# ReLU-squared attention and a SwiGLU feed-forward on one core: 64x64 tiles for gate, value and score products

## The chip, the cores and the metric

The kernel runs on one core of a Trainium2 chip. The metric is device time in microseconds (us) of one execution; lower is better. The engines of the core run side by side: PE (TensorE, matrix products into PSUM), DVE (VectorE), ACT (ScalarE), POOL (GpSimd) and SP (SyncE, which here only starts transfers). PE has two kinds of instruction, a weight load (PEld in the profile) and a matmul (PE).

A matmul here multiplies a stationary operand (`lhsT`, loaded as weights) with a moving one (`rhs`) and writes `lhsT.T @ rhs`. It need not fill PE's 128x128 array. The rows it takes are the partitions of its operands, the columns are the partitions of its output. A 64x128 tile takes half of the rows and all of the columns, so two of them, one on the upper rows and one on the lower rows, can run at the same time. A 64x64 tile takes a quarter of the array, and four can run at the same time.

## The reference, cut to what matters

```python
# q, k, v: (8, 12, 448, 64) float32: batch, heads, sequence, head dimension
scores = scale * np.matmul(q, k.transpose(0, 1, 3, 2))
attn = np.maximum(scores, 0.0) ** 2 / S
a = np.matmul(attn, v)
x = a.transpose(0, 2, 1, 3).reshape(B * S, H * D)      # 3584 x 768
xn = x / np.sqrt(np.mean(x * x, axis=-1, keepdims=True) + 1e-6) * rms_g
g = xn @ w_gate                                         # 768 -> 1536
silu = g * (1.0 / (1.0 + np.exp(-g)))
out = (silu * (xn @ w_val)) @ w_out                     # 1536 -> 768
```

## The kernel before

Everything is computed in bfloat16 with float32 sums. The eight batches follow each other. While the feed-forward part of batch b runs, the attention of batch b+1 is worked in between, unit by unit. Batch 0's attention has nothing to be put beside and comes first, with some filler matmuls (`keep_busy`, psB).

**Attention units** (`attention`). `scores` makes the products of one chunk of 128 keys for two heads. The head dimension is 64, so each head takes one half of the rows: two matmuls on 64x128 tiles with 448 columns, into psS (line 212 of the profile). `rest_scores` (line 227) makes the last 64 keys of two pairs of heads on four 64x64 tiles. `rectify` takes ReLU on ACT or DVE and the square on DVE. `attend` makes attention times V for two pairs of heads into psAV on four 64x64 tiles (line 258): a first pass of four steps, `rest_scores` for another pair between the passes in most calls, then a second pass of three steps that adds to what the first pass wrote from the other half of the rows. An empty instruction with a dependence on the first pass's matmuls stands ahead of the second, so that the two halves do not add to the same place at once.

**The feed-forward part** is a list of groups. `projection` is a gate or value product of 128 hidden features for 448 tokens: six steps (KT) over the 768 inputs, into a PSUM buffer psP. `outproj` makes three `Piece`s for 128 tokens, each of 256 output columns and twelve steps (FT), into psO. `norm_sums` (psSS) has the shape of a projection and makes the sums of squares for the next batch. All of these are written by one line, 380, in `Group.emit`.

Each group of n steps is cut at its contraction: a step has an upper half (partitions 0 to 63 of the operands, upper rows of the array) and a lower half (partitions 64 to 127, lower rows), so each group needs 2n matmuls that add into the same PSUM buffer. `Stream.step` issues one **slot**: at most one matmul for the upper half of a group called *lead*, and one for the lower half of another group called *follow*. A gate or value group usually does its six upper halves first, as lead, and then its six lower halves, as follow, while the next group leads. A group that changes from one half to the other must not have both in PE at once. Two things see to it: `ready` refuses a group that changes its half before `APART` = 2 steps have gone by, and `emit` places an empty instruction (`nc.tensor.nop`) that depends on the group's last matmul. In the built program that dependence is a semaphore wait on the weight load that comes next.

```python
        def ready(self, half):
            if self.last not in (None, half) and self.rest < stream.APART:
                return False
            return self.count[half] < (self.count[0] if half else self.bound())
```

`rest` is set to 0 by a group's own slot and goes up by one at the end of every slot, so between a group's last upper half and its first lower half there is at least one slot of other groups. A `Piece` does its twelve steps in two runs of six upper and six lower halves. A slot may hold two groups of different kinds, for example psSS as lead and psO as follow.

**Order.** `manual_schedule` keeps the order in which the code issues instructions on each engine. The main loop spreads the next batch's attention units over the slots of the current batch by a list of costs. When a group has all its steps, ACT makes SiLU of a gate (line 451), DVE multiplies it with the value (line 456), and ACT copies psO out (line 490), from where SP stores it.

Of the kernel before, what the change touches and what calls it, by code (L numbers as in the profile page):

```python
# [20 lines left out]
def kernel(  # L21
# [11 lines left out]
    nc = tc.nc  # L33
    P = nc.NUM_PARTITIONS
    B, H, S, D = q.shape
    T, DM = out.shape
    _, F = moe_w_gate.shape
    assert (T, DM) == (B * S, H * D) and 2 * D == P and S % NCH == 0 and B % 2 == 0 and S == U * D
    PC = S // NCH
    KT, FT, HP = DM // P, F // P, H // 2  # L40
# [23 lines left out]
    qkT = {}  # L64
# [3 lines left out]
    def load(nm, b, h0=0, h1=H):  # L68
        runs = nm == "v" or b < PE_T
        n, w = (PC, NCH) if nm == "q" else (P, UH)  # L70
        if (nm, b) not in ld:
            shape = [n, H, w * D] if runs else [n, w, H * D]
            ld[nm, b] = ldpool.tile(shape, BF16, name=nm + "b", tag=nm + "b")
            if nm == "k" and runs:
                nc.vector.memset(ld[nm, b][D:, :, (UH - 1) * D :], 0.0)
        t = ld[nm, b]
        src = src_of[nm][b, h0:h1]
        if nm == "q":
            parts = [(slice(0, PC), PC, 0, NCH)]
        else:  # L80
            parts = [(slice(0, D), D, 0, UH), (slice(D, P), D, UH if nm == "k" else UH - 1, U)]
        for prt, n, u0, u1 in parts:
            if runs:
                nc.gpsimd.dma_start(  # L84
                    out=t[prt, h0:h1, : (u1 - u0) * D],
                    in_=src.rearrange("h (p u) d -> p h (u d)", p=n)[:, :, u0 * D : u1 * D],
                )
            else:
                to = t[prt].rearrange("p u (h d) -> p u h d", d=D)
                rows = src.rearrange("h (p u) d -> p u h d", p=n)  # L90
                step = u1 - u0 if nm == "q" else 1
                for u in range(u0, u1, step):
                    nc.gpsimd.dma_start(  # L93
                        out=to[:, u - u0 : u - u0 + step, h0:h1, :], in_=rows[:, u : u + step]
                    )
# [70 lines left out]
    behind = mybir.DependencyInfo(mybir.DependencyClass.Sync, mybir.DependencyReason.DATA)  # L166
# [30 lines left out]
    def rectify(b, j, c, psS):  # L197
        r = apool.tile([P, 2, S], BF16, name="r", tag="r")
        if relu_on(b, j, c) == "dve":
            nc.vector.tensor_relu(out=r[:], in_=psS[:, :, :S])  # L200
        else:
            nc.scalar.activation(out=r[:], in_=psS[:, :, :S], func=ACT.Relu)  # L202
        eng = nc.gpsimd if square_on(b, j, c) == "pool" else nc.vector
        flush()
        pending.append(lambda: eng.tensor_tensor(out=r[:], in0=r[:], in1=r[:], op=ALU.mult))  # L205
        rsq[b, j, c] = r

    def scores(b, j, c):
        psS = ps_s.tile([P, 2, 512], FP32, name="psS", tag="psS")
        for hh in range(2):  # L210
            prt = slice(hh * D, (hh + 1) * D)
            nc.tensor.matmul(  # L212
                out=psS[:, hh, :S],
                lhsT=qkT[b][prt, j, 0, c * P : (c + 1) * P],
                rhs=qkT[b][prt, j, 1, :],
                start=True,
                stop=True,
            )
        rectify(b, j, c, psS)

    def rest_scores(b, j):
# [59 lines left out]
    def attention(b):  # L281
        units = []

        def add(cost, *fns):
            units.append((cost, lambda: [f() for f in fns]))

        if b < PE_T:
            add(0.4, lambda: transposes(b, 0))
            add(0.4, lambda: transposes(b, 1))
            add(0.3, lambda: rectify(b, 0, UH - 1, rest_scores(b, 0)))  # L290
        for j in range(HP):
            for c in range(UH - 1):
                if c == 2 and j in (2, 4):
                    add(1.6, lambda j=j: attend(b, j - 2, (b, j)))
                add(0.3, lambda j=j, c=c: scores(b, j, c))
                if c == 1 and b < PE_T and j + 2 < HP:
                    add(0.4, lambda j=j: transposes(b, j + 2))
                if b == 0:
                    add(0.3, lambda: keep_busy(1))
        add(0.1, flush)  # L300
        add(1.6, lambda: attend(b, HP - 2, (b + 1, 0) if PE_T <= b + 1 < B else None), flush)
        return units
# [3 lines left out]
    class Stream:  # L306
# [28 lines left out]
        def step(self):  # L335
            if not (self.todo or self.open):
                return False
            lead = self.pick(0, None)
            follow = self.pick(1, lead)
            for half, g in ((0, lead), (1, follow)):  # L340
                if g is not None:
                    g.emit(half)
            self.at = [lead, follow]
            for g in self.open:
                g.rest += 1
            if follow is not None and follow.count[1] == follow.n:
                self.open.remove(follow)
                follow.done(follow.ps)
            return True
# [7 lines left out]
    class Group:  # L357
# [14 lines left out]
        def begin(self):  # L372
            self.ps = ps_m.tile([P, 512], FP32, name=self.name, tag="mm")

        def emit(self, half):
            i = self.count[half]
            prt = slice(half * D, (half + 1) * D)
            if self.last not in (None, half):
                tc.add_manual_dep(nc.tensor.nop().ins, self.mm.name, behind)
            mm = nc.tensor.matmul(  # L380
                out=self.ps[:, : self.w], lhsT=self.lhsT(i)[prt], rhs=self.rhs(i)[prt],
                start=(half == 0 and i == 0), stop=(half == 1 and i == self.n - 1),
            )
            self.count[half] += 1
            self.last, self.rest = half, 0
            self.mm = mm.ins

    class Piece(Group):

# [190 lines left out]
```

## Time and profile before

Three runs took 466.82, 468.20 and 469.97 us. One execution was profiled:

| | us or share |
|---|---|
| median of the runs | 468.2 |
| span of the profiled execution, first to last instruction | 466.5 |
| matmuls and weight loads on PE | 5722 each |
| psP matmuls, 64x128 tiles, 448 columns | 2268 (1140 value, 1128 gate), 0.349 each |
| psO matmuls, 64x128 tiles, 256 columns | 2016, 0.271 each |
| psS matmuls on 64x128 tiles | 288, 0.358 each |
| psAV matmuls, 64x64 tiles | 672, 0.361 each |
| psS matmuls on 64x64 tiles | 96, 0.360 each |
| mean weight load, 64x128 | 0.094 |
| mean weight load, 64x64 | 0.106 |

The duration of a matmul in the profile is from its start to the modelled end of its result. Matmuls overlap: the next on the same rows starts before the one ahead of it has ended, so the time of a slot is read from starts, not from durations. A line of the timeline gives start, length, engine, line of the kernel, operation, output and inputs, shape, and how many instructions of the same kind were merged into it; brackets at its end give idle time before it and what ended it. In "64*128 64x448" the first pair is the tile on the array, the second the partitions and columns of the moving operand. "PEld" lines are weight loads; a load with a wait appears when the wait is over.

### The profile page before, as it was taken

How to read it: one execution, taken by the hardware profiler on the slowest of the kernel's cores; microseconds unless marked ns; L12 is line 12 of the kernel's file. 1: busy time of each engine (PE TensorE's matmuls, PEld its weight loads, DVE VectorE, ACT ScalarE, POOL GpSimd, SP SyncE). 2: the span in 40 equal slices, each digit the busy share in tenths (PEclk: the TensorE clock that was granted, in tenths of full speed). 3: DMA queues.
4: the chain of work that ended last, by engine and by line, in shares of the span. 5: the costliest groups of instructions: out<-in, count | busy, mean ns of one | idle time of the engine just before them, and what ended most of it. 6: DMA issues, size and time to landing. Idle time of an engine off the chain costs nothing.

```text
span 466.5 us, 12798 instructions
## 1 busy us (share of the span) xinstructions
PE 453.6 (97%) x5722; PEld 292.8 (63%) x5722; DVE 274.0 (59%) x403; ACT 234.9 (50%) x360; POOL 80.6 (17%) x97
## 2 busy tenths in 40 slices
PE   6989999999999999999999999999999999999995
PEld 3434655676666766676666766676667766676674
DVE  1676378866663867576566657576656677332200
ACT  1682246665645655375445755465535764532221
POOL 8438211571007000340007000100000000000000
PEclk8698999999999999999999999999999999999998
DMA  9999999799907970299209960438002200020013
GB/s 106 194 204 199 206 173 162 80 204 165 127 3 107 214 124 2 23 200 146 44 1 124 211 109 1 58 82 135 20 1 54 85 2 1 2 84 20 1 42 95
DMA packets 130758, 44.47 MB, mean 95 GB/s; under 512 B 102928, under 2 KB 127120, under 8 KB 130704
## 3 DMA queue, kind: packets, MB, share of 16 engines
q0 software_dynamic: 91648, 24.39, 54.1%
q1 hardware_dynamic: 39056, 19.28, 20.5%
q8 instruction: 44, 0.72, 0.6%
q14 instruction: 10, 0.08, 0.0%
HBM read 48.76 MB, written 11.01 MB: 128 GB/s over the span
## 4 chain that ended last, share of the span: by engine, by line
PE 91%; DVE 3%; ACT 2%; DMA 1%; POOL 1%; issue 1%; POOLq 0%
PE psP L380 47%; PE psO L380 23%; PE psAV L258 8%; PE psS L212 6%; PE psSS L380 2%; ACT r L202 2%; PE psB L140 1%; PE psT L177 1%; PE psS L227 1%; DMA kb<-in_k_dram 1%; DVE xn L427 1%; PE psP L441 1%; DVE r L200 1%; DVE r L205 1%; DVE rstd L424 1%
## 5 line engine op out<-in xcount | busy, mean ns | idle before, releaser
L380 PE MATMUL psP<-xn,wv_sb 64*128 64x448 bf16 x1140 | 229.0, 349 | 0.0
L380 PE MATMUL psP<-xn,wg_sb 64*128 64x448 bf16 x1128 | 227.8, 349 | 0.1
L380 PE MATMUL psO<-wo_sb,hT 64*128 64x256 bf16 x2016 | 139.6, 271 | 0.0
L202 ACT ACTIVATE r<-psS 128x896 bf16<-128x896 f32 x123 | 111.1, 918 | 47.5 <-PE psS L212 46.8
L380 PEld LDWEIGHTS <-wv_sb 64*128 64x128 bf16 x1140 | 96.1, 94 | 41.5 <-issue 4.3
L380 PEld LDWEIGHTS <-hT 64*128 64x128 bf16 x2016 | 101.1, 94 | 33.0 <-issue 2.9
L380 PEld LDWEIGHTS <-wg_sb 64*128 64x128 bf16 x1128 | 94.3, 94 | 35.6 <-issue 1.3
L205 DVE TENSOR_TENSOR r<-r 128x896 bf16<-128x896 bf16 x165 | 100.9, 628 | 16.3 <-ACT r L202 15.6
L456 DVE TENSOR_TENSOR hT<-sil,psP 128x448 bf16<-128x448 bf16 x96 | 59.5, 620 | 79.7 <-PE psP L380 52.4
L451 ACT ACTIVATE sil<-psP 128x448 bf16<-128x448 f32 x96 | 51.9, 542 | 74.7 <-PE psP L380 68.8
L200 DVE TENSOR_SCALAR r<-psS 128x896 bf16<-128x896 f32 x45 | 49.1, 1090 | 31.7 <-PE psS L227 24.2
L212 PE MATMUL psS<-qkT 64*128 64x448 bf16 x288 | 59.3, 358 | 1.9 <-DVE r L200 1.2
L490 ACT COPY ost<-psO 128x256 f32<-128x256 f32 x84 | 30.5, 372 | 43.5 <-PE psO L380 39.6
L276 ACT ACTIVATE xT<-psAV 128x896 bf16<-128x896 f32 x24 | 22.0, 917 | 54.4 <-PE psAV L258 50.1
L258 PE MATMUL psAV<-r,vb 64*64 64x448 bf16 x672 | 43.9, 361 | 1.8 <-POOL r L205 1.2
L84 POOL DMA_DIRECT2D vb<-in_v_dram x18 | 13.2, 750 | 167.7 <-PE psO L380 122.3
L424 DVE RECIPROCAL rstd<-rstd 128x448 f32<-128x448 f32 x8 | 23.6, 2953 | 26.0 <-ACT rstd L420 26.0
L93 POOL DMA_DIRECT2D kb<-in_k_dram x42 | 33.0, 1008 | 18.7 <-DMA wo_sb<-in_moe_w_out_dram 9.6
L258 PEld LDWEIGHTS <-vb 64*64 64x64 bf16 x672 | 17.3, 106 | 22.3 <-issue 10.3
L427 DVE SCALAR_TENSOR_TENSOR xn<-xT,g_sb,rstd 128x448 bf16<-128x448 bf16 x48 | 29.3, 680 | 0.3
L212 PEld LDWEIGHTS <-qkT 64*128 64x128 bf16 x288 | 19.8, 94 | 11.4 <-issue 6.2
L140 PE MATMUL psB<-busy_bf,ones_bf 128*128 128x448 bf16 x58 | 17.6, 418 | 1.3 <-DVE busy_bf L135 1.3
(38 smaller groups left out, 161.7 us busy)
## 6 DMA issues: line engine op xcount, KB each, us to landing
vb<-in_v_dram POOLq DMA_DIRECT2D x14, 384.0 KB, 7.2
qb<-in_q_dram POOLq DMA_DIRECT2D x7, 672.0 KB, 12.9
kb<-in_k_dram POOLq DMA_DIRECT2D x43, 96.0 KB, 12.7
out_dram<-ost SPq DMA_DIRECT2D x8, 336.0 KB, 4.1
wg_sb<-in_moe_w_gate_dram POOLq DMA_DIRECT2D x4, 576.0 KB, 16.5
wv_sb<-in_moe_w_val_dram POOLq DMA_DIRECT2D x4, 576.0 KB, 18.1
wo_sb<-in_moe_w_out_dram POOLq DMA_DIRECT2D x2, 1152.0 KB, 21.4
out_dram<-ost SPq DMA_DIRECT2D x8, 288.0 KB, 4.4
```

The source lines that it names most:

```text
L93: nc.gpsimd.dma_start(out=to[:, u - u0 : u - u0 + step, h0:h1, :], in_=rows[:, u : u + step])
L200: nc.vector.tensor_relu(out=r[:], in_=psS[:, :, :S])
L202: nc.scalar.activation(out=r[:], in_=psS[:, :, :S], func=ACT.Relu)
L205: pending.append(lambda: eng.tensor_tensor(out=r[:], in0=r[:], in1=r[:], op=ALU.mult))
L212: nc.tensor.matmul(out=psS[:, hh, :S], lhsT=qkT[b][prt, j, 0, c * P : (c + 1) * P], rhs=qkT[b][prt, j, 1, :], start=True, stop=True,)
L258: mm = nc.tensor.matmul(out=psAV[hh * D : (hh + 1) * D, jj, :S], lhsT=v[prt, 2 * (j + jj) + hh, u * D : (u + 1) * D], rhs=r[prt, hh, :], s ...
L380: mm = nc.tensor.matmul(out=self.ps[:, : self.w], lhsT=self.lhsT(i)[prt], rhs=self.rhs(i)[prt], start=(half == 0 and i == 0), stop=(half = ...
L424: nc.vector.reciprocal(out=rstd[:], in_=rstd[:])
L427: nc.vector.scalar_tensor_tensor(out=xn[:, kt, :], in0=xTs[b][:, kt, :], scalar=g_sb[:, kt : kt + 1], in1=rstd[:], op0=ALU.mult, op1=ALU.mult,
L451: nc.scalar.activation(out=s[:], in_=psG[:], func=ACT.Silu)
L456: nc.vector.tensor_tensor(out=hTs[b // 2][:, fb, o : o + S], in0=sil[b, fb][:], in1=psV[:], op=ALU.mult)
L490: nc.scalar.copy(out=ost[:, o : o + w], in_=ps[:, :w])
```

## The change

The `scores` products and every slot that contains a gate, a value or a sum-of-squares group are issued as 64x64 tiles: each matmul of 128 output rows becomes two, one for output partitions 0 to 63 and one for 64 to 127. Within a slot the order is: first block of lead, first block of follow, second block of lead, second block of follow. Slots of output projection alone stay on two 64x128 tiles, and so do the scores that come between them: the flag `quarters` holds what the last slot was. An output projection that shares its slot with a psP or psSS group is quartered too.

`emit` is divided into three. `ordered` places the empty instruction for a change of halves, `emit` the matmul of one block, `emitted` keeps the count. `step` calls `ordered` for lead and follow, then `emit` for all blocks, then `emitted`. The last matmul that the dependence names is that of the second block.

```diff
--- before.py
+++ after.py
@@ -205,17 +205,23 @@
         pending.append(lambda: eng.tensor_tensor(out=r[:], in0=r[:], in1=r[:], op=ALU.mult))
         rsq[b, j, c] = r
 
+    quarters = [True]
+
+    def blocks():
+        return ((0, D), (D, P)) if quarters[0] else ((0, P),)
+
     def scores(b, j, c):
         psS = ps_s.tile([P, 2, 512], FP32, name="psS", tag="psS")
-        for hh in range(2):
-            prt = slice(hh * D, (hh + 1) * D)
-            nc.tensor.matmul(
-                out=psS[:, hh, :S],
-                lhsT=qkT[b][prt, j, 0, c * P : (c + 1) * P],
-                rhs=qkT[b][prt, j, 1, :],
-                start=True,
-                stop=True,
-            )
+        for m0, m1 in blocks():
+            for hh in range(2):
+                prt = slice(hh * D, (hh + 1) * D)
+                nc.tensor.matmul(
+                    out=psS[m0:m1, hh, :S],
+                    lhsT=qkT[b][prt, j, 0, c * P + m0 : c * P + m1],
+                    rhs=qkT[b][prt, j, 1, :],
+                    start=True,
+                    stop=True,
+                )
         rectify(b, j, c, psS)
 
     def rest_scores(b, j):
@@ -337,9 +343,15 @@
                 return False
             lead = self.pick(0, None)
             follow = self.pick(1, lead)
-            for half, g in ((0, lead), (1, follow)):
-                if g is not None:
-                    g.emit(half)
+            pair = [(half, g) for half, g in ((0, lead), (1, follow)) if g is not None]
+            quarters[0] = any(g.n == KT for _, g in pair)
+            for half, g in pair:
+                g.ordered(half)
+            for m in blocks():
+                for half, g in pair:
+                    g.emit(half, *m)
+            for half, g in pair:
+                g.emitted(half)
             self.at = [lead, follow]
             for g in self.open:
                 g.rest += 1
@@ -372,18 +384,23 @@
         def begin(self):
             self.ps = ps_m.tile([P, 512], FP32, name=self.name, tag="mm")
 
-        def emit(self, half):
+        def ordered(self, half):
+            if self.last not in (None, half):
+                tc.add_manual_dep(nc.tensor.nop().ins, self.mm.name, behind)
+
+        def emit(self, half, m0, m1):
             i = self.count[half]
             prt = slice(half * D, (half + 1) * D)
-            if self.last not in (None, half):
-                tc.add_manual_dep(nc.tensor.nop().ins, self.mm.name, behind)
             mm = nc.tensor.matmul(
-                out=self.ps[:, : self.w], lhsT=self.lhsT(i)[prt], rhs=self.rhs(i)[prt],
+                out=self.ps[m0:m1, : self.w], lhsT=self.lhsT(i)[prt, m0:m1],
+                rhs=self.rhs(i)[prt],
                 start=(half == 0 and i == 0), stop=(half == 1 and i == self.n - 1),
             )
+            self.mm = mm.ins
+
+        def emitted(self, half):
             self.count[half] += 1
             self.last, self.rest = half, 0
-            self.mm = mm.ins
 
     class Piece(Group):
 
```

## Prediction

> **What bounds the kernel now.** I read the page first: the busy shares (part 1), the granted clock, then the chain that ended last (part 4).
>
> ```profile
> span 466.5 us, 12798 instructions
> PE 453.6 (97%) x5722; PEld 292.8 (63%) x5722; DVE 274.0 (59%) x403; ACT 234.9 (50%) x360; POOL 80.6 (17%) x97
> PE 91%; DVE 3%; ACT 2%; DMA 1%; POOL 1%; issue 1%; POOLq 0%
> ```
>
> 91% of the chain is PE; of it psP (gate and value) is 47% and psO (output projection) 23%. DVE and ACT have 40 and 50% of slack. So the question is how long one *slot* of PE takes, and whether the change touches that. The chain in order of time, in a gate/value stage, says how long it is (start, length, what):
>
> ```profile
> 160.51 1.32 PE psP L380 x14
> 161.84 0.19 PE psS L212 x2
> 162.02 1.32 PE psP L380 x14
> 163.35 0.19 PE psS L212 x2
> ```
>
> Fourteen psP matmuls are seven slots of two: 1.32/7 = 0.189 us a slot. A score slot takes 0.19 too. The windows view grants a clock of 1.00 from 40 us to the end; 448 columns at 0.189 us is as fast as any row of this trace streams, and psO's 256 columns keep the same proportion with 0.109. Next, the timeline of PE around one attention-times-V, the only place where four 64x64 tiles run now:
>
> ```profile
> 165.98 0.35 PE L380 MATMUL psP<-xn,wv_sb 64*128 64x448 bf16 x1
> 166.03 0.35 PE L380 MATMUL psP<-xn,wg_sb 64*128 64x448 bf16 x1
> 166.31 0.95 PE L258 MATMUL psAV<-r,vb 64*64 64x448 bf16 x16
> 167.09 0.36 PE L227 MATMUL psS<-qkT 64*64 64x448 bf16 x4
> 167.32 0.79 PE L258 MATMUL psAV<-r,vb 64*64 64x448 bf16 x12
> 168.04 0.36 PE L380 MATMUL psP<-xn,wv_sb 64*128 64x448 bf16 x1
> 168.05 0.36 PE L380 MATMUL psP<-xn,wg_sb 64*128 64x448 bf16 x1
> 168.25 0.35 PE L380 MATMUL psP<-xn,wv_sb 64*128 64x448 bf16 x1
> ```
>
> Four 4-tile slots run from 166.31 to 167.09, 0.78 us: three at 0.19 and a first one of 0.21. So a slot costs the same with two tiles or four. Around them stand the switches: 166.03 to 166.31 is 0.28 where a slot is 0.19, and 0.02 more on the first slot; going back, 12 matmuls are three slots, so the last starts near 167.76, and 167.76 to 168.04 is again 0.28. A switch of tile shape costs about 0.10 to 0.11 us. And 167.09 to 167.32 is 0.23, not 0.19: the second pass of attention-times-V waits for the matmuls of the first, with one slot between.
>
> Last, what a wait for the other half's matmuls costs in the stream. First the timeline of a psP group going over (lines from PE and PEld), then psO's in three short windows:
>
> ```profile
> 160.31 0.35 PE L380 MATMUL psP<-xn,wg_sb 64*128 64x448 bf16 x1
> 160.71 0.09 PEld L380 LDWEIGHTS <-wg_sb 64*128 64x128 bf16 x1
> 160.73 0.35 PE L380 MATMUL psP<-xn,wg_sb 64*128 64x448 bf16 x1
> ...
> 406.22 0.62 PE L380 MATMUL psO<-wo_sb,hT 64*128 64x256 bf16 x8
> 406.56 0.10 PEld L380 LDWEIGHTS <-hT 64*128 64x128 bf16 x2
> ...
> 407.24 0.10 PEld L380 LDWEIGHTS <-hT 64*128 64x128 bf16 x2
> ```
>
> The gate group's last upper-half matmul starts at 160.31; the held weight load of its lower half goes at 160.71, 0.40 to 0.41 later (0.35 of matmul and some 0.06 to be told). In psO it is 406.22 to 406.56: 0.33 to 0.34. Two slots are 0.378 and 0.218: the release comes later than the slot that wants it. Today this is nearly free, because only the lower half is held and it runs behind the upper one: by 0.04 us in psP (165.98 against 166.03 above), by a whole slot in psO. psO's held loads return every 0.68 us, six slots, against 6 x 0.109 = 0.655: 0.025 a wait, the load that comes late. In psP the 1.32 us stretches contain such waits and show no loss.
>
> **The change, part by part.** Counts come from the instruction order of the two built kernels; the other four engines keep theirs exactly.
>
> *Twice the instructions in a slot.* PE gets 2769 more weight loads and as many matmuls. I take nothing for them: in the attention-times-V rows they lie within the 0.19 us. What covers them is the stream of 448 columns itself. Bounds: 0 from that row. The other end is issue: eight instructions in 0.189 us are 23.6 ns each, and the longest stretch at that pace now is one attention-times-V; for longer, the fastest is psO, four in 0.109, 27.3 ns. Were that the limit, a slot would be 0.218, and 1134 psP, 42 psSS and 120 score slots would cost 1296 x 0.029 = 38 us. psO is bound by its own columns, so its pace is no sign of a limit: I take 0. The weight loads are longer by the rows, 94 ns at 64x128 and 106 at 64x64, both hidden under 189.
> [...]
>
> *Switches of tile shape.* 31 go between psP and attention-times-V (16 in, 15 out), and a few between attention units. But the output projection now has another shape than what lies around it: 33 boundaries inside the stream of psP, psSS or a mixed slot with a pure psO slot become switches, and in all the order has 105 before and 107 after. 2 x 0.1 = +0.2 us. If the new boundaries were free, it would be 31 x 0.105 = 3.3 us saved; no row excludes it, I take the +0.2, since the drain is that of the matmul before.
> [...]
>
> *The waits move to the head of the slot.* This is the part that costs. `ordered` places the waits of both halves ahead of the slot's first load, where `emit` placed the follower's after the leader's load and matmul. PE takes loads in order, so behind the held load stand all loads and matmuls of the slot, the leader's too, and then every score and attention slot. The lag between halves, which hid the release, can't form: the upper half is now held at each group change, and each such hold is paid in full.
> psP: 141 waits with one slot between. The awaited matmul is third of four and starts about 0.005 after its slot; 0.005 + 0.405 + 0.002 = 0.412 against 0.378 is 0.035, and the slot after it is a first one, +0.02 to 0.025 for loads that could not go ahead: 0.06. The nearest row says the same: 167.09 to 167.32, 0.04 over a slot, and 0.02 behind it. 141 x 0.059 = 8.3 us. Another 36 have a score slot between (0.567, over 0.412): free.
> psO: 132 waits with one slot between: 0.335 + 0.005 - 0.218 = 0.12, and 0.01 for the late loads, 0.13, less the 0.025 paid now: 0.105. 132 x 0.105 = 13.9 us. The 61 with five slots between are free.
> Bounds: nothing if some lag absorbs them; above, if a whole load of 0.106 showed each time, 141 x 0.08 + 132 x 0.08 = 22 us more. I take the rows that are the same event.
> What is late next: SiLU on ACT, the product on DVE and the copies of psO wait for PE as today, by engines with 40% of slack; no new wait follows. The weight and input loads have landed in time already.
>
> **Sum.** 466.5 + 0 + 0.2 + 8.3 + 13.9 = 488.9 us for the execution profiled. The three runs have a median of 468.2, 1.7 above that span (the lowest, 466.8, 0.3 above): 488.9 + 1.7 = 490.6, say 490.5.
>
> **Rivals.** (A) *The drains were the cost and the waits are free*: if the loads behind a held one still go ahead, or the two row halves find a lag as now, the slot keeps 0.189 and the 31 drains at attention-times-V are a gain as the new boundaries fall on stalls already there: 468.2 - 3.3 = 465. For it: the lag exists today. Against: two loads at 406.56 start together, the second held by the first, and in the 4-tile rows all four tiles stand still until 167.32. It decides where the release is below two slots, 0.378 and 0.218; measured are 0.405 and 0.335. (B) *Issue becomes the bound*: 27.3 ns an instruction, 38 us, in which psP's waits vanish (two slots are then 0.437, more than 0.412): 468.2 + 38 + 13.9 = 520. For it: no stretch longer than an attention-times-V goes faster. Against: nothing idles there. (C) *Only psP pays*: psO keeps its shape and, if the lower half keeps its lag of a slot, also its 0.113: 468.2 + 8.3 + 0.2 = 477. Against: the upper half itself is held now.
>
> **How the numbers follow.** Forecast 0.78, its own range 484 to 498: from waits without the late load (141 x 0.035 + 132 x 0.095 = 17.5 us, 486) less a little of the drains, to half a load more. A 0.07, B 0.07, C 0.08. With C's 477 and the forecast's range some 8 in 10 are inside: 476 to 498. A measurement of this kernel can tell about 1% (4.7 us) from no change: the three runs spread by 0.7%. A's 465 lies 0.7% below, so it is within 1% a little more often than beyond: faster 0.03, same 0.04, slower 0.93.
>
> **What would show it.** In the changed profile a gate/value stage should read 0.189 a slot with 0.22 to 0.23 and then 0.21 at each group change, all four tiles together, instead of an even row; psO six slots in about 0.78 us instead of 0.68; no extra gap between psP and psAV, and 0.28 between psP and psO. PE stays near 97% busy, and ACT and DVE keep their sums. An even slot of 0.21 to 0.22 throughout means (B); psO at 0.68 means (C); no longer rows at the group changes, (A), and my reading of the held load is wrong.

## The result, and the profile after

| | before | after |
|---|---|---|
| median, us | 467.5 | 495.1 (494.42 to 496.80, 4 runs) |
| ratio | 1 | 1.0579, 95% interval 1.0541 to 1.0617 |
| span of the profiled execution | 466.5 | 492.6 |
| first gate/value matmul of the stream starts at | 48.91 | 47.35 |
| from there to the end of the span ("stream" below) | 417.6 | 445.3 |

The kernel is 5.8% slower, 27.6 us. The forecast was 490.5 (476 to 498). What comes before the stream differs from run to run (it starts between 46.2 and 51.9 us in the traces below), so kernels are compared below by the stream as well as by the median.

The page of the changed kernel: span, busy time by engine, the lines of the chain that ended last, and the queue of instruction fetches.

```profile
span 492.6 us, 18336 instructions
PE 475.6 (97%) x8491; PEld 274.6 (56%) x8491; DVE 274.6 (56%) x403; ACT 235.8 (48%) x360; POOL 80.6 (16%) x97
PE psP L394 47%; PE psO L394 27%; PE psAV L264 7%; PE psS L218 6%; PE psSS L394 2%; ACT r L202 1%; PE psB L140 1%; PE psT L177 1%; PE psS L233 1%; DMA kb<-in_k_dram 1%; PE psP L458 1%; DVE r L200 0%; DVE r L205 0%; ACT xT L282 0%; POOL qb L84 0%
q8 instruction: 66, 1.08, 0.9%
```

PE is as busy as before, 97%, and DVE and ACT keep their sums (274.0 and 234.9 before). The busy share can't show the loss: matmuls that wait still overlap the one before. psO's part of the chain rose from 23% to 27% although slots of output projection alone kept their two tiles. The timeline of PE and PEld in a gate/value stage shows where a slot became longer (start, length, engine; one or two lines of each slot):

```profile
185.95 0.79 PE L394 MATMUL psP<-xn,wv_sb 64*64 64x448 bf16 x6
186.37 0.10 PEld L394 LDWEIGHTS <-wv_sb 64*64 64x64 bf16 x1 [0.30 <-PE psP L394]
186.37 0.37 PE L394 MATMUL psP<-xn,wg_sb 64*64 64x448 bf16 x1
186.58 0.35 PE L394 MATMUL psP<-xn,wv_sb 64*64 64x448 bf16 x1
186.77 0.35 PE L394 MATMUL psP<-xn,wv_sb 64*64 64x448 bf16 x1
...
188.36 0.35 PE L394 MATMUL psP<-xn,wv_sb 64*64 64x448 bf16 x1
188.54 0.93 PE L264 MATMUL psAV<-r,vb 64*64 64x448 bf16 x16
```

At 186.37 a group changes its half. The load's bracket names psP's own matmuls as what ended its idle time, and all four tiles start only then. The slots' own starts in this trace are 0.189 apart as a rule, and here 0.235, then 0.213 (186.37 to 186.58), then 0.19 again. The step from psP to psAV is now an ordinary slot, 0.18 to 0.19, where it was 0.28. The output projection late in the run, PEld's timeline:

```profile
427.84 0.55 PEld L394 LDWEIGHTS <-hT 64*128 64x128 bf16 x12 [0.23 <-PE psO L394]
428.62 0.55 PEld L394 LDWEIGHTS <-hT 64*128 64x128 bf16 x12 [0.23 <-PE psO L394]
429.39 0.55 PEld L394 LDWEIGHTS <-hT 64*128 64x128 bf16 x12 [0.23 <-PE psO L394]
```

Six slots take 0.78 us, where the held loads before came back after 0.68. Last, something that the profile before did not have: three places in the first batch on the stream where PE waits for nothing that the profile can name.

```profile
113.97 0.35 PE L394 MATMUL psP<-xn,wg_sb 64*64 64x448 bf16 x1
114.80 0.35 PE L394 MATMUL psP<-xn,wv_sb 64*64 64x448 bf16 x1 [0.48 <-issue]
...
123.19 0.35 PE L394 MATMUL psP<-xn,wv_sb 64*64 64x448 bf16 x1 [1.79 <-issue]
...
131.03 0.35 PE L394 MATMUL psP<-xn,wg_sb 64*64 64x448 bf16 x1 [1.31 <-issue]
```

Counted from start to start less a slot, these cost 0.64, 1.95 and 1.47 us, and one at 71 us in attention-times-V another 0.63: 4.7 us. The packets in the trace show a 16 KB instruction fetch just ahead of each of the three, at 112.4, 120.2 and 128.3 us. The kernel before has no such stop in its stream.

### The profile page after: what moved, and what is told of

Its sections match the earlier page's. It is cut to its first block, busy times and chain, and to the rows that moved or that the text cites. A ratio compares the mean times of both kernels' runs of the same rounds, so it can differ in the third digit from the quotient of the medians.

```text
span 492.6 us, 18336 instructions
## 1 busy us (share of the span) xinstructions
PE 475.6 (97%) x8491; PEld 274.6 (56%) x8491; DVE 274.6 (56%) x403; ACT 235.8 (48%) x360; POOL 80.6 (16%) x97
## 4 chain that ended last, share of the span: by engine, by line
PE 93%; ACT 2%; issue 1%; DVE 1%; DMA 1%; POOL 1%; POOLq 0%
PE psP L394 47%; PE psO L394 27%; PE psAV L264 7%; PE psS L218 6%; PE psSS L394 2%; ACT r L202 1%; PE psB L140 1%; PE psT L177 1%; PE psS L233 1%; DMA kb<-in_k_dram 1%; PE psP L458 1%; DVE r L200 0%; DVE r L205 0%; ACT xT L282 0%; POOL qb L84 0%
## 5 line engine op out<-in xcount | busy, mean ns | idle before, releaser
L394 PE MATMUL psP<-xn,wv_sb 64*64 64x448 bf16 x2280 | 240.7, 353 | 2.3 <-issue 2.3
L394 PE MATMUL psP<-xn,wg_sb 64*64 64x448 bf16 x2256 | 238.6, 353 | 1.3 <-issue 1.3
L394 PE MATMUL psO<-wo_sb,hT 64*128 64x256 bf16 (+1 forms) x2193 | 150.9, 272 | 0.0
L394 PEld LDWEIGHTS <-wv_sb 64*64 64x64 bf16 x2280 | 110.3, 106 | 53.0 <-PE psP L394 21.7
L394 PEld LDWEIGHTS <-wg_sb 64*64 64x64 bf16 x2256 | 108.6, 106 | 52.4 <-PE psP L394 20.1
L394 PEld LDWEIGHTS <-hT 64*128 64x128 bf16 (+1 forms) x2193 | 96.2, 96 | 52.0 <-PE psO L394 35.1
L205 DVE TENSOR_TENSOR r<-r 128x896 bf16<-128x896 bf16 x165 | 101.2, 628 | 22.9 <-ACT r L202 22.1
L468 ACT ACTIVATE sil<-psP 128x448 bf16<-128x448 f32 x96 | 51.9, 542 | 82.9 <-PE psP L394 75.1
L218 PE MATMUL psS<-qkT 64*64 64x448 bf16 (+1 forms) x528 | 55.0, 360 | 1.9 <-DVE r L200 1.4
L264 PE MATMUL psAV<-r,vb 64*64 64x448 bf16 x672 | 42.9, 354 | 2.1 <-POOL r L205 1.2
L84 POOL DMA_DIRECT2D vb<-in_v_dram x18 | 13.2, 749 | 176.0 <-PE psO L394 123.7
L441 DVE RECIPROCAL rstd<-rstd 128x448 f32<-128x448 f32 x8 | 23.6, 2952 | 29.4 <-ACT rstd L437 29.4
L93 POOL DMA_DIRECT2D kb<-in_k_dram x42 | 33.0, 1009 | 24.0 <-DMA vb<-in_v_dram 10.6
L264 PEld LDWEIGHTS <-vb 64*64 64x64 bf16 x672 | 19.2, 106 | 18.0 <-PE psAV L264 7.2
L218 PEld LDWEIGHTS <-qkT 64*64 64x64 bf16 (+1 forms) x528 | 18.2, 106 | 12.0 <-issue 5.6
```

What stands on the lines that cost most here:

```text
L93: nc.gpsimd.dma_start(out=to[:, u - u0 : u - u0 + step, h0:h1, :], in_=rows[:, u : u + step])
L218: nc.tensor.matmul(out=psS[m0:m1, hh, :S], lhsT=qkT[b][prt, j, 0, c * P + m0 : c * P + m1], rhs=qkT[b][prt, j, 1, :], start=True, stop=True,)
L264: mm = nc.tensor.matmul(out=psAV[hh * D : (hh + 1) * D, jj, :S], lhsT=v[prt, 2 * (j + jj) + hh, u * D : (u + 1) * D], rhs=r[prt, hh, :], s ...
L394: mm = nc.tensor.matmul(out=self.ps[m0:m1, : self.w], lhsT=self.lhsT(i)[prt, m0:m1], rhs=self.rhs(i)[prt], start=(half == 0 and i == 0), s ...
L441: nc.vector.reciprocal(out=rstd[:], in_=rstd[:])
L468: nc.scalar.activation(out=s[:], in_=psG[:], func=ACT.Silu)
```

## The experiments

Two theories stood against each other. W: the waits at the head of the slot make the loss (and the stops are something else). F: the four tiles do, by their instructions, loads and switches.

**e1, each half's wait back ahead of that half alone, tiles as after.**

```diff
-            for half, g in pair:
-                g.ordered(half)
-            for m in blocks():
-                for half, g in pair:
-                    g.emit(half, *m)
+            for half, g in pair:
+                g.ordered(half)
+                for m in blocks():
+                    g.emit(half, *m)
```

> The changed kernel with each half's wait placed ahead of that half alone, as before the change: a slot is now both blocks of lead, then the wait, then both blocks of follow. Tiles, counts (8491 matmuls) and switches of shape (107) stay. Theory W (the waits at the head of the slot cost 8.3 us in psP and 13.9 us in psO; some 4 us are three stops of PE around 114, 121 and 129 us for which the profile names no releaser; four tiles cost nothing): 495.1 - 22 = 473, up to 479 if the lag between the halves has to be drained at each switch of shape; psO at about 0.68 us for six slots again. Rival F (four tiles cost, by their instructions, loads and switches): it stays at 490 to 495.

Measured: 477.88 (476.19 to 479.04), ratio 1.0225 (1.0187 to 1.0263), stream 428.4. Of the 27.6 us, 17 go by putting the wait back (and with it the order of the four blocks), with all 8491 matmuls in place: F falls. What is left over the kernel before, 10.8 us of stream, is mostly stops: 6.7 us by the same count, the longest 2.97 at 114.6 us, and after that one the windows view shows the clock (the column after POOL) at half:

```profile
118.00:121.00 3.00, 3.00 (x38) 1.96 (x30) 0.62 (x1) 0.00 (x0) 0.00 (x0) 0.50 1.71 150
121.50:124.50 3.00, 3.00 (x69) 2.79 (x64) 2.93 (x5) 2.21 (x3) 0.00 (x0) 1.00 2.63 131
```

38 matmuls in 3 us where 69 follow. The clock record of the trace has the half from 118.0 to 121.4 us, which costs some 1.7 us. Some 2.4 us of e1 remain that no line was found for; that a lag between the halves is lost again at each switch of shape is an argument, not shown.

**e2, two tiles everywhere, only the waits at the head.** `quarters` is never true.

```diff
-    quarters = [True]
+    quarters = [False]
...
-            quarters[0] = any(g.n == KT for _, g in pair)
+            quarters[0] = False
```

> The changed kernel with the flag quarters always false: two 64x128 tiles everywhere as before the change (5722 matmuls, 105 switches), and only the waits of both halves at the head of the slot. Theory W: psP 141 x (0.035 + 0.011) = 6.5 and psO 132 x 0.105 = 13.9 us over the kernel before, 467.5 + 20.4 = 488, with no stops of a microsecond on PE around 114 to 130 us. Rival F: 467 to 470, since the four tiles are gone.

Measured: 486.20 (483.38 to 486.46), ratio 1.0392 (1.0351 to 1.0433), stream 435.4, 17.8 over the kernel before, and no stop by issue. The waits alone, without a single new tile, make two thirds of the loss. Its output projection has the period of the changed kernel (PEld's timeline):

```profile
425.55 0.55 PEld L394 LDWEIGHTS <-hT 64*128 64x128 bf16 x12 [0.23 <-PE psO L394]
426.32 0.55 PEld L394 LDWEIGHTS <-hT 64*128 64x128 bf16 x12 [0.23 <-PE psO L394]
```

In psP its long slots are 0.22 and then 0.20, some 145 of them, against 0.235 and 0.213 on four tiles: the slot whose loads could not go ahead is longer by 0.011 at 64x128 and by 0.024 at 64x64. The held load itself goes 0.405 us after the start of the matmul it waits for on two tiles, and 0.416 on four (medians of both traces). With 0.042 for each pair of long slots psP's waits make 6.1 of e2's 17.8 us, and 11.7 are left for psO.

**e3, one more slot of rest: APART = 3 in the changed kernel.**

> The changed kernel with APART = 3 in place of 2: a group rests for two slots of others before it changes its half, so a wait at the head finds 3 x 0.189 = 0.567 us (needed 0.412) in psP and 3 x 0.109 = 0.327 (needed 0.340) in psO. 17 matmuls more than the changed kernel has, 105 switches. Theory W: psP's 8.3 us go whole and of psO's wait 0.013 and the late load of 0.011 stay, 132 x 0.024 = 3.2, what the kernel before pays too: 495.1 - 8.3 - 13.9 = 473, 468 to 474. Rival F: 490 to 495, for tiles, instructions and switches stay.

Measured: 473.58 (471.38 to 477.43), ratio 1.0137 (1.0065 to 1.0209), stream 423.6. The 6.0 us over the kernel before equal its stops, 6.0 by the same count; the longest three in the timeline of PE:

```profile
116.62 0.35 PE L394 MATMUL psP<-xn,wv_sb 64*64 64x448 bf16 x1 [1.39 <-issue]
124.46 0.35 PE L394 MATMUL psP<-xn,wv_sb 64*64 64x448 bf16 x1 [1.35 <-issue]
132.58 0.38 PE L394 MATMUL psP<-xn,wv_sb 64*64 64x448 bf16 x4 [1.82 <-issue]
```

A constant that only sets the distance between two halves takes back 21.5 us of median. That what is left equals the stops is partly chance, since the longer rest also helps psO: some 145 of its slots take 0.12 us, some 250 in the kernel before.

**e5, the wait back at the follower in slots of pure output projection only.**

```diff
+            if not quarters[0]:
+                for half, g in pair:
+                    g.ordered(half)
+                    g.emit(half, 0, P)
...
```

> The changed kernel with the wait put back ahead of follow alone in slots of pure output projection; slots of four tiles keep both waits at the head. Theory W: psO's 13.9 us go and psP's 8.3 stay: 495.1 - 13.9 = 481, psO at about 0.68 us for six slots, psP with 0.22 and 0.21 at the group changes. Rival F: 490 to 495.

Measured: 484.55 (484.49 to 486.26), ratio 1.0379 (1.0346 to 1.0413), stream 432.0. By the stream e5 is 445.29 - 432.03 = 13.3 us faster than the changed kernel, but not all of that is psO's waits, since its trace also has fewer stops. The waits view (engine and what it works on, what ended the wait: idle us in total, times, longest), two lines of the changed kernel and one of e5:

```profile
PE psP L394 <- issue: 3.6, 3, 1.8
PE psAV L264 <- issue: 0.5, 1, 0.5
...
PE psP L399 <- issue: 2.9, 2, 1.5
```

By the count above these are 4.7 and 3.2 us. Without the 1.5 us between them psO's waits are 11.7, as in e2. By the median e5 gains 10.6, less than expected; the stream of this profiled run also begins 3.4 us later, at 50.75.

**g1 to g4, the same pairs with light transfers.** So far the waits were settled; open were the stops. Theory I: an instruction fetch is late behind crowded transfers. J: the doubled instructions stop PE whatever the transfers do. In g1 to g4 q and k of all batches are transposed on PE and no DMA transpose is left; with that the loads have long runs for all batches: from 108 to 134 us g2 has 164 packets, 32 of them under 512 B, and the changed kernel 17082, of which 16561 are under 512 B.

```diff
-    PE_T = 2
+    PE_T = B
...
-    def transpose_dma(b):
...
-            side.insert(len(side) // 2, (0, lambda b=b: transpose_dma(b + 2)))
```

g1, on the kernel before:

> The kernel before with the q and k of all batches transposed on PE (PE_T = 8), no DMA transposes, and with that the loads of all batches in long runs of memory: the transfers get light, PE gets 576 transposes more, 36 units of 16, each some 0.55 us and two switches, 0.8 in all: 467.6 + 29 = 497. It is the measure for g2. Both theories expect the same, and hardly a stop on PE.

g2, on the changed kernel:

> The changed kernel with PE_T = 8, so with g1's transfers. The changed kernel is 27 us over the kernel before: some 22 by the waits and 4 to 5 by three stops of PE next to instruction fetches between 113 and 132 us. Theory I (the fetches are late behind crowded transfers): with the DMA transposes and the short runs gone the stops of over 0.6 us go, and g2 - g1 is the waits alone, 19 to 22. Rival J (the stops come with the doubled instructions, whatever the transfers do): the stops are there in the first batch on the stream, g2 - g1 = 25 to 28.

g3, g1 with APART = 3:

> g1 with APART = 3: two 64x128 tiles. The kernel before pays some 0.025 us at each of 145 psO waits for a load that comes late; a slot more of rest lets it go ahead: g1 - 3.6 if a pair is still found for every slot. It is the measure for g4.

g4, g2 with APART = 3:

> g2 with APART = 3: four tiles, no waits that bind in psP. Theory W with I: four tiles in themselves cost nothing and no stop is left, so g4 lies within 3 us of g3. Theory W with J: g3 + 5 to 8, with the stops. Rival F (four tiles cost by their loads and issue): g3 + 10 or more, spread over the slots, psP over 0.195 a slot.

| | median | ratio to the kernel before | stream |
|---|---|---|---|
| g1, two tiles | 503.55 | 1.0754 (1.0708 to 1.0800) | 454.3 |
| g2, four tiles, waits at the head | 520.10 | 1.1118 (1.1084 to 1.1152) | 469.2 |
| g3, two tiles, APART 3 | 503.60 | 1.0762 (1.0728 to 1.0795) | 454.0 |
| g4, four tiles, APART 3 | 505.03 | 1.0791 (1.0748 to 1.0835) | 453.3 |

g1 is 6 us slower than expected; its PE stops for up to 2.6 us before transposes, which all four share in some measure and which were not followed up. The clock differs as well. It stands at 0.50 for two stretches of 3.4 us in g1 (from 165.9 and 224.0), two in g4 (from 167.1 and 225.2) and 10.2 us in all in g3, and never in g2's stream. One line of the windows view each (stretch, length, busy time of PE, PEld, DVE, ACT, POOL with counts, clock, DMA share, GB/s), of g1, g3 and g4:

```profile
166.00:169.30 3.30, 3.30 (x20) 1.98 (x18) 1.75 (x3) 1.37 (x3) 0.00 (x0) 0.50 0.00 0
104.50:111.20 6.70, 6.70 (x51) 4.30 (x51) 2.34 (x3) 0.77 (x3) 0.00 (x0) 0.50 0.15 40
167.20:170.50 3.30, 3.30 (x42) 2.29 (x45) 0.96 (x2) 0.37 (x1) 0.00 (x0) 0.50 0.00 0
```

g2 - g1 is 16.6 us by the medians and 14.9 by the stream: below the 19 to 22 of I, and far from the 25 to 28 of J. But g1 has some 2.7 us more of those stops and loses some 3.4 us to the clock; with both the waits are 21 us, inside I's range. g4 and g3 can't be told apart (1.4 us, the intervals overlap; -0.7 by the stream). Stops and clock put aside (some 1.8 and 1.7 us more in g3), g4's slots are some 2.8 us longer, of which 2.6 stand in slots of output projection alone, on two tiles in both kernels: some 150 of these take 0.12 us in g4, where the wait is at the head, and some 20 in g3. So four tiles without binding waits cost next to nothing here. g3 did not gain the 3.6 us over g1. The long psO slots are gone from it (some 20 against some 250), but the gain is lost among stops and clock. The stretch of the stops, in the windows view of three kernels, first the changed kernel:

```profile
108.00:134.00 26.00, 22.41 (x445) 14.00 (x442) 13.96 (x23) 12.17 (x17) 2.90 (x4) 1.00 1.69 131
```

e2, two tiles with the same transfers:

```profile
108.00:134.00 26.00, 26.00 (x298) 11.57 (x296) 17.12 (x28) 14.49 (x20) 0.75 (x1) 1.00 1.48 106
```

g2, four tiles with light transfers:

```profile
108.00:134.00 26.00, 26.00 (x532) 15.15 (x526) 17.16 (x27) 14.28 (x20) 0.00 (x0) 1.00 0.06 18
```

Idle time on PE in this stretch appears only where four tiles and crowded transfers (a DMA share of 1.69) meet: 22.41 busy of 26. Two tiles under the same load and four tiles without it run through. So J falls as well for slots of gate and value. Crowding alone is not enough either: from 166 to 170 us of the changed kernel the share is 1.72, and PE is busy throughout. That the stops belong to the fetches shows in their ends: at all 21 pauses by issue of the changed kernel, e1, e3, e5 and g5 (below), the shortest among them too, PE goes on 1.2 to 1.8 us after the last fetch's packet has ended, only at e1's longest 2.8. Whether and how the transfers delay them is not shown: the three packets took 0.94 to 1.35 us, and one at 192.8, where nothing stopped, 1.48. Which transfers matter, the short runs or the DMA transposes, wasn't separated.

**e8, the kernel before with APART = 3 and the loads moved to the middle of each batch.**

> The kernel before with APART = 3 and with the loads and transposes moved as in e7: the control for e7, on two tiles. [...] If it is faster than e4 by 3 us or more, moving the loads helps by something other than the fetches.

No time was measured for e4 (the kernel before with APART = 3 alone), e7 (e3 with the loads moved) and e6 (e3 with the output projection on four tiles). So what moved loads do to the stops of the changed kernel is open. Measured for e8: 466.10 (464.98 to 467.42, 12 runs), ratio 0.9970 (0.9952 to 0.9989), stream 415.9: the fastest of all, by 0.3%. The long psO slots are gone (6 of 0.12 us against some 250), but of 3.6 us only 1.7 came through, and without e4 the two edits can't be told apart.

**g5, g4 with the output projection on four tiles too.**

```diff
-            quarters[0] = any(g.n == KT for _, g in pair)
+            quarters[0] = True
```

> g4 with the flag quarters always true: the output projection on four 64x64 tiles too, 10954 matmuls instead of 9104, 57 switches of shape fewer. A psO slot has eight instructions in 0.109 us, 13.6 ns each, for stages of some 15 us. Theory I (the pace of issue is no limit at 23.6 ns; only a late fetch stops PE): 57 x 0.1 = 5.7 us off, 505 - 5.7 = 499, if 13.6 ns hold as well. Rival P (issue binds near 24 ns): a psO slot takes 0.19 instead of 0.109, 1008 x 0.08 = 81 us more, 586. In between, with psO slots of 0.12 to 0.15: issue or the fetches bind at that pace but not at 23.6 ns, 510 to 540.

Measured: 500.63 (499.57 to 501.23), ratio 1.0686 (1.0661 to 1.0711), 4.4 us less than g4. The chain in order of time:

```profile
439.97 7.86 PE psO L382 x272
```

272 matmuls are 68 slots: 0.116 us a slot, eight instructions in it, 14.4 ns each, for 7.86 us on end. The pace of issue is no limit at 23.6. Four stops by issue, 3.9 us of idle time, are in its psO stages, each next to a fetch, and three of the four with few transfers in flight. The windows view around them:

```profile
97.00:101.00 4.00, 2.13 (x71) 1.59 (x67) 3.96 (x5) 1.18 (x5) 0.00 (x0) 1.00 1.11 252
157.00:160.00 3.00, 2.70 (x92) 2.06 (x84) 2.96 (x4) 1.28 (x4) 0.00 (x0) 1.00 0.05 15
273.00:276.00 3.00, 2.20 (x76) 1.70 (x66) 3.00 (x6) 0.37 (x1) 0.00 (x0) 1.00 0.45 127
488.00:491.00 3.00, 2.04 (x72) 1.55 (x68) 0.00 (x0) 1.01 (x3) 0.00 (x0) 1.00 0.17 40
```

So in these runs crowded transfers were needed for a stop at 23.6 ns an instruction, but not at 14.4.

## Why the prediction was right, and what it lacked

- *A slot costs the same with two tiles or four*: right. Slots of the changed kernel are 0.189 where nothing waits, and g4 can't be told from g3.
- *The waits at the head cost 8.3 us in psP and 13.9 in psO*: right in kind, and shown by e1, e2, e3 and e5. psO came out at 11.7 (e5's stream without the stops, and e2). Its six slots take the 0.78 us that was forecast, which is 132 x 0.10 = 13.2; where the other 1.5 us are won was not followed up. psP was sized low: 0.059 a wait was forecast, 0.046 + 0.024 = 0.070 measured, 141 x 0.070 = 9.9. The step "0.005 + 0.405 + 0.002 = 0.412" is the one: the two slots take 0.189 + 0.235 = 0.424, as on four tiles the release comes 0.416 us after the start of the awaited matmul, and that starts 0.007 after its slot.
- *Switches of shape: +0.2*: the 0.28 us between psP and psAV went as forecast, and 0.29 appeared between psP and psO (200.60 to 200.89 in the trace). What a switch waits for is the matmul ahead of it: in both traces the next shape starts 0.28 us after the start of a psP, psSS or psAV matmul (448 columns) and 0.20 to 0.21 after that of a psO matmul (256; to psAV, 200.89 to 201.10 in the trace after), in both cases 0.07 before its modelled end. That the drains nearly cancel was not tested in the changed kernel alone. g5, with 57 switches fewer than g4, is 4.4 us faster, 5.7 expected, but this is no clean test: g5 also has stops by issue and psO slots of 0.116 instead of 0.109, and g4 alone loses some 3.4 us at half the clock.
- *Twice the instructions: 0, or 38 us if issue binds*: here the prediction lacked a term. The pace does not bind (g5), so rival B was wrong as it stood. But I weighed instructions by their pace alone and not by how they arrive: 8491 pairs need 66 fetches instead of 44, and PE stops next to four of them, one at 71 us and three between 113 and 131. That is 4.7 us in the trace after, and nothing before.
- *Fetches*: 66 packets of 16 KB for 16982 loads and matmuls are some 257 a packet, where the kernel before has 44 for 11444, some 260. Outside the output projection only kernels with four tiles in psP stop by issue. Why PE stops under crowded transfers with eight instructions in a slot (e3, a share of 1.42 from 112 to 134 us) and not with four (e2, 1.48 from 108 to 134 us), no run shows.
- *The sum*: 11.7 (psO) + 11.2 (e5 over the kernel before, its stops taken off: psP's waits and the switches) + 4.7 = 27.6, against 27.7 of stream. As the first two both come from e5's trace, that the sum closes is no test; by the slots psP's waits are 9.9, and the 1.3 that are left of the 11.2 have no line. Forecast were 22.4 us: the stops were missing with 4.7, psP and the switches were 2.7 too low, and psO 2.2 too high. That the last two nearly cancel is luck.
- *Rivals*: A (waits free, drains saved) falls by the long slot at 186.37; C (only psP pays) by the period of 0.78; B by the slots of 0.189 in the changed kernel, and by g5.

## What to carry to other kernels

Where two streams of accumulation share a slot of the instruction order, a wait belongs ahead of the one instruction that needs it, not at the slot's head: ahead of the slot it takes from both the lag that hid it, and costs with two tiles (17.8 us in e2) most of what it costs with four (22.9 without the stops). Compare the release time (here 0.405 to 0.416 and 0.33 us after the matmul's start) with the distance in slots (0.378 and 0.218) before placing it; one slot more of distance was worth 21.5 us. And work cut into more and smaller instructions should be checked against the arrival of instructions: at 23.6 ns an instruction PE stopped only where transfers crowded, at 14.4 also where they did not (g5), and the slots look free in every stretch between.

## What the runs showed of the hardware that was not expected

- PE stopped for up to 2.97 us (e1) in the middle of a stream next to an instruction fetch, waiting for nothing that the profile names, when transfers of short runs and DMA transposes were in flight (DMA share 1.69 in the changed kernel), and did not with a share of 0.06 (g2). At 14.4 ns an instruction it stopped with a share of 0.05 as well (g5).
- After the longest stop (idle 2.81 us, e1) PE's clock stood at 0.50 from 118.0 to 121.4 us, so that a stop of 3 us cost over a microsecond more. After the stops of 1.3 to 1.8 us in the changed kernel and e3 it stayed at 1.00. The length of a stop does not settle it: in g4, among transposes, the clock went to 0.50 at the end of 1.82 us of idle time (167.1), and in g3 it stayed at 1.00 after 2.15 us (167.5).
- PE took eight instructions in 0.116 us, 14.4 ns each, for almost 8 us (g5).
